# Weights' scales from column sums on TensorE, sign images for two pieces at a time

## The chip, the cores and the metric

The kernel runs on one core of a Trainium2 chip. The metric is the device time of one execution in microseconds, the median of the runs shown. The core's engines have an instruction queue each: TensorE (PE, with its weight loads shown apart as PEld), VectorE (DVE), ScalarE (ACT), GpSimd (POOL), and SyncE (SP), which issues the DMAs. TensorE writes PSUM, the others read it.

## The reference

```python
B, H, S, D, C = 4, 8, 768, 64, 16          # batch, heads, tokens, head size, clusters
# attention: a query sees only keys whose nearest centroid is its own
q_assign = argmax(einsum('bhsd,hcd->bhsc', q_n, c_n))      # the same for k
scores = where(q_assign == k_assign, (q @ k.T) / sqrt(D), -1e9)
x = softmax(scores) @ v                                    # -> (B, S, 512)
# Fourier mixing and a feed-forward layer
u = x + real(fft(fft(x, axis=1), axis=2))
un = (u - mean(u)) / sqrt(var(u) + 1e-6)
out = u + maximum(un @ w_ch1, 0) @ w_ch2                   # w_ch1 512x2048, w_ch2 2048x512
```

All inputs and the output are float32.

## The kernel before

TensorE works on 16-bit operands, so every float32 matrix is split into a high and a low half of 16 bits (`hi` and `lo`), after it was scaled by a power of two, and a product takes three matmuls.

**Attention** (class `Attention`) goes over 16 pairs of heads, four for each batch entry. A pair has six steps `st`, one for each 128 queries. `scores(pr, st)` makes two tiles `ps_big` of 128x768 in PSUM (two is all there are, so the next step has to wait until both are read): 12 matmuls (L320) and four that add the cluster mask (L325). For each of the two heads VectorE scales a tile and takes its row minimum (L339, output `ju` or, for batch 0, `X`), ScalarE takes the exponential (L345; L343 for batch 0) and its 16-bit half (L353), GpSimd the low half (L354), and SyncE transposes both by DMA into `pt` (L356). `attend` multiplies `pt` with the values into the one tile `ps_o` (L374 to L376), and every third step `finish` scales that tile into `X` on VectorE (L386, L388, L390). `prep` loads and splits q and k of a later pair in nine parts, with `along` (L48) for maxima over partitions and a one-hot code that is transposed by DMA (L303).

**Weights** (class `Weights`, the object of the change): the two matrices come in 32 pieces of 128x512, 16 each, loaded into eight buffers `RAW`, read in halves of 16 bits. Each iteration `k` of `run` does one part for several pieces:
- `load`: a DMA of 512 KB.
- `largest` (L491): VectorE takes each row's largest magnitude from the top 16 bits of the numbers; for the first matrix, four pieces' maxima are joined (L496), spread over partitions by a matmul with the identity (`along`) and reduced again (L504), so that one scale holds for four pieces; for the second each row has its own scale.
- `top_power` (L58 to L61): four small VectorE operations turn maxima into a power of two `s` and its inverse `inv`.
- `signs` (L519, L520): ScalarE makes from the top 16 bits an image of the positive numbers and one of the negative ones, in one of two buffers `PN`.
- `join` (L528, L532): two matmuls with plus and minus the identity put the images together as float32 in a tile `ps_f` (of which there are three, shared with all else but scores and `ps_o`), and VectorE adds the low bits.
- `halve`: ScalarE makes the high half (L538), and VectorE (L544) or ScalarE and GpSimd (L541, L542) the low one.

`relative` then brings the scales of both matrices together in `rel` and `dsc`.

**Fourier** and **FeedForward** follow for a finished batch entry: `fold` adds and subtracts the halves of `X` (L660) and their mirror images (L661) and splits the result; `transform` multiplies it with tables; `up` (L858) and `down` (L888) are the two products with the weights.

**Order.** `Overlap.run` writes a table of calls by step number: attention is the backbone; the 41 parts of `Weights.run` are dealt out at 0.684 steps each from step 0, the first scores come at step 5, and batch 0 ends at step 29. The Fourier and feed-forward work of entry `b` is dealt out between the steps of entry `b + 1`; that of the last entry runs by itself at the end. TensorE takes its instructions in the order of this table; on the other engines a scheduler orders them when the kernel is built.

Of the kernel before, what the change touches and what calls it, by code (L numbers as in the profile page):

```python
# [25 lines left out]
P = 128  # L26
# [28 lines left out]
def top_power(nc, tops, s, inv):  # L55

    t = tops.bitcast(I32)
    nc.vector.tensor_scalar(out=t, in0=t, scalar1=20, scalar2=None, op0=ALU.logical_shift_right)  # L58
    nc.vector.tensor_scalar(out=t, in0=t, scalar1=-910.0, scalar2=1.0, op0=ALU.add, op1=ALU.max)
    nc.vector.tensor_scalar(out=inv.bitcast(I32), in0=t, scalar1=240.0, scalar2=float(1 << 23), op0=ALU.min, op1=ALU.mult)  # L60
    nc.vector.reciprocal(out=s, in_=inv)  # L61
# [20 lines left out]
class Attention:  # L82
# [226 lines left out]
    def scores(self, pr, st):  # L309
        nc, sb = self.nc, self.sb  # L310
        assert self.ready >= pr
        (hq, hk), oh, (e, ne) = self.hl[pr], self.oht[pr], self.sc.scores(pr)
# [14 lines left out]
        for j in range(2):  # L327

            m = sb.tile([P, 1], F32, name="rmx", tag="rmx", bufs=6)
            early = pr < H // 2  # L330
            if early:

                n = (2 * st + j) % self.RING * S
                p32 = self.X[1].rearrange("p a x -> p (a x)")[:, n:n + S]
            else:
                p32 = sb.tile([P, S], F32, name="p32", tag="p32", bufs=2)
            x = p32.rearrange("p (h x) -> p h x", h=2)
            ju = x if early else sb.tile([P, 2, SH], BF16, name="ju", tag="ju")
            self.mark = nc.vector.tensor_scalar(out=ju, in0=ps[j][:, :, 0:SH], scalar1=ne, scalar2=None, op0=ALU.mult, op1=ALU.min,  # L339
                                    accum_out=m)  # L340
            self.late = m
            if early:
                nc.scalar.activation(p32, p32, AF.Exp, bias=m, scale=-1.0)  # L343
            else:
                nc.scalar.activation(x, ps[j][:, :, 0:SH], AF.Exp, bias=m, scale=e)  # L345
            if early and j:
                ph = sb.tile([P, S], F32, name="p32", tag="p32", bufs=2).bitcast(F16).rearrange("p (a x) -> p a x", a=2)
            else:
                ph = sb.tile([P, 2, S], F16, name="ph", tag="ph", bufs=2)
            if early and j and (st in self.PC):  # L350
                nc.gpsimd.tensor_copy(out=ph[:, 0], in_=p32)
            else:
                nc.scalar.copy(out=ph[:, 0], in_=p32)  # L353
            nc.gpsimd.tensor_tensor(out=ph[:, 1], in0=p32, in1=ph[:, 0], op=ALU.subtract)  # L354
# [79 lines left out]
class Weights:  # L434
# [7 lines left out]
    RAW, PN = tuple(4128 * i for i in range(6)) + (29696, 33824), (24768, 26816)  # L442
    ID, TOP, MX = 28864, 29376, 29472
# [3 lines left out]
    def __init__(self, tc, pool, arena, psf, w1, w2, ident):  # L447
# [6 lines left out]
        self.inv = [pool.tile([P, n], F32, name=f"winv{n}") for n in (4, 16)]  # L454
# [31 lines left out]
    def largest(self, k):  # L486

        nc, at = self.nc, self.arena.at
        g, i = divmod(k, 4)
        mx = at(self.MX + 32 * (g % 2), [P, 4], F32)  # L490
        nc.vector.tensor_reduce(out=mx[:, i:i + 1], in_=self.top(k).bitcast(BF16), op=ALU.max, axis=AX.X,  # L491
                                apply_absolute_value=True)
        if i == 3 and g >= 4:
            self.scales(g, mx)
        elif i == 3:
            nc.vector.tensor_reduce(out=mx[:, 0:1], in_=mx, op=ALU.max, axis=AX.X)  # L496

    def block(self, g):

        nc, at = self.nc, self.arena.at  # L500
        mx = at(self.MX + 32 * (g % 2), [P, 4], F32)
        ps = self.psf()
        along(nc, ps[:, 0:P], mx[:, 0:1], self.ident)
        nc.vector.tensor_reduce(out=mx[:, 1:2], in_=ps[:, 0:P], op=ALU.max, axis=AX.X)  # L504
        self.scales(g, mx[:, 1:2])

    def scales(self, g, mx):
        n = mx.shape[1]
        s = self.sb.tile([P, 4], F32, name="wsc", tag="wsc", bufs=2)
        top_power(self.nc, mx, s[:, 0:n], self.inv[0][:, g:g + 1] if n == 1 else self.inv[1][:, 4 * (g - 4):4 * (g - 3)])  # L510
        for i in range(4):
            self.scale[4 * g + i] = s[:, i % n:i % n + 1]

    def signs(self, k):

        nc, at = self.nc, self.arena.at
        pn = at(self.PN[k % 2], [P, 2, DM], BF16)
        top = self.top(k)
        nc.scalar.activation(pn[:, 0].bitcast(I16), top.bitcast(I16), AF.Relu, bias=self.off[:, 0:1], scale=8.0)  # L519
        nc.scalar.activation(pn[:, 1].bitcast(I16), top, AF.Relu, bias=self.off[:, 1:2], scale=8.0)  # L520
        self.bits[k] = pn
# [24 lines left out]
    def run(self):  # L546
# [5 lines left out]
        for i in range(2):  # L552
            nc.gpsimd.tensor_scalar(out=self.idb[:, i], in0=self.ident, scalar1=1.0 - 2 * i, scalar2=None, op0=ALU.mult)
        for k in range(-self.AHEAD, 33):
# [16 lines left out]
    def relative(self):  # L571

        nc, at = self.nc, self.arena.at
        top, m1, r = (at(self.TOP + 32 * j, [P, 1], F32) for j in range(3))
        rel = self.rel
        nc.vector.tensor_tensor(out=rel.rearrange("p (a c) -> p a c", c=4),
                                in0=self.inv[1].rearrange("p (a c) -> p a c", c=4),
                                in1=self.inv[0].rearrange("p (a o) -> p a o", o=1).broadcast_to([P, 4, 4]), op=ALU.mult)
        nc.vector.tensor_reduce(out=m1, in_=rel, op=ALU.max, axis=AX.X)
        ps = self.psf()  # L580
        along(nc, ps[:, 0:P], m1, self.ident)
        nc.vector.tensor_reduce(out=top, in_=ps[:, 0:P], op=ALU.max, axis=AX.X)
        nc.vector.reciprocal(out=r, in_=top)
        nc.vector.tensor_scalar(out=rel, in0=rel, scalar1=r[:, 0:1], scalar2=HSC, op0=ALU.mult, op1=ALU.mult)
# [36 lines left out]
class Fourier:  # L621
# [11 lines left out]
    FE = (0, 0, 0, 1)  # L633
# [13 lines left out]
    def fold(self, b):  # L647
# [5 lines left out]
        mid = at(self.XM, [1, M + 1], F32)  # L653
        nc.gpsimd.tensor_copy(out=mid, in_=X[0:1, 3, 0:M + 1])
        nc.gpsimd.tensor_tensor(out=mid[:, 1:M], in0=mid[:, 1:M], in1=X[0:1, 3, DM - 1:M:-1], op=ALU.add)
        last = at(self.XL, [P, 3], F32)
        xt = {}
        for i, op in self.FOLDS:
# [9 lines left out]
            xt[i] = t.rearrange("p (a t c) x -> p a t c x", a=2, t=3)  # L668
        self.parts[b] = xt, last, mid, s
# [119 lines left out]
HSC = float(2.0 ** -20)  # L789
# [111 lines left out]
class Overlap:  # L901
# [23 lines left out]
    PIN, PF, PV = (), 29, 1  # L925
    CE, WP, WQ = 0.45, 0, 0

    def layer(self, b, old):
# [13 lines left out]
        yield from old  # L942
        for blk in range(3):
            for f, cost in enumerate(ffn.up(blk)):
                if blk == 0 and f == 0:
# [116 lines left out]
def cluster_attention_fourier_ffn_kernel(ctx, tc, q, k, v, cent, w1, w2, cd, sd, cm, cs, ss, ny, out):  # L1062
# [6 lines left out]
    arena = Arena(glob, 47264)  # L1069
# [47 lines left out]
```

## Time and profile before

| | |
|---|---|
| runs | 1053.73, 1049.66, 1053.15 us; median 1053.15 |
| profiled execution | 1049.91 us, span 1048.1 us |
| busy share | TensorE 87%, VectorE 60%, ScalarE 60%, GpSimd 56% |
| mean granted TensorE clock | 0.949 |
| batch 0 beside the weights | from the first scores to the last weight piece, 31 to 192 us |
| last entry alone | from about 860 us |

Times in the profile are microseconds from the span's start. A group's row gives line, engine, operation, output and inputs with their shapes, the count, then busy time and mean ns of one, then the engine's idle time just before and what ended it. A busy engine is not always at its peak, and idle time of an engine on which nothing waits costs nothing.

### The profile page before, as it was taken

To read this page: it belongs to the slowest core of one execution; us is meant where nothing else is said; L and a number is where in the kernel's file an instruction comes from. 1 tells how busy PE (TensorE), PEld (TensorE's weight loads), DVE (VectorE), ACT (ScalarE), POOL (GpSimd) and SP (SyncE) were. 2 spreads that over 40 slices of the span, in tenths; PEclk is the share of its full clock that TensorE was granted. 3 is DMA by queue.
4 is the path that set the end of the run, shared out by engine and by line. 5 is a ranking of instruction groups with operands and counts; after the bars stand their busy time and mean duration, and the time that the engine had idled before them with its cause. 6 is when DMAs were issued, how large, how long until landed. Compare 5 with 4: busy or idle time off the path is not lost.

```text
span 1048.1 us, 23542 instructions
## 1 busy us (share of the span) xinstructions
PE 910.8 (87%) x9350; PEld 591.7 (56%) x9362; DVE 627.4 (60%) x1297; ACT 625.3 (60%) x980; POOL 586.9 (56%) x693
## 2 busy tenths in 40 slices
PE   3665565749899999998899999997999999999998
PEld 2333333425575756655666757555757667576674
DVE  8789899767757555668656555667555333631110
ACT  4798889755766665645666746556756543351230
POOL 2364565753975756655856646647847645271230
PEclk9987878769899999999899999998999999999999
DMA  7799998979887776568877767588757562321000
GB/s 272 179 225 245 196 239 166 171 156 153 177 123 153 128 154 121 121 137 161 153 137 142 140 128 132 110 141 170 124 102 133 96 110 43 81 52 31 11 11 21
DMA packets 396239, 140.01 MB, mean 134 GB/s; under 512 B 381784, under 2 KB 381792, under 8 KB 396128
## 3 DMA queue, kind: packets, MB, share of 16 engines
q1 hardware_dynamic: 396128, 138.50, 65.9%
q8 instruction: 73, 1.20, 0.5%
q14 instruction: 38, 0.31, 0.1%
HBM read 42.52 MB, written 6.29 MB: 47 GB/s over the span
## 4 chain that ended last, share of the span: by engine, by line
PE 39%; DVE 6%; DMA 3%; ACT 3%; POOL 2%; issue 2%; SPq 0%; ACTq 0%; DVEq 0%; POOLq 0%
PE ps_f L888 16%; PE ps_f L858 13%; PE ps_big L320 3%; DMA pt<-ph 3%; PE ps_f L713 2%; DVE ju L339 1%; ACT p L345 1%; PE ps_o L374 1%; POOL ph L354 1%; PE ps_o L375 1%; PE ps_o L376 1%; PE ps_big L325 1%; ACT ph L353 1%; DMA scr<-in_k_dram 0%; DVE arena L660 0%
## 5 line engine op out<-in xcount | busy, mean ns | idle before, releaser
L354 POOL TENSOR_TENSOR ph<-p,ph 128x768 f16<-128x768 f32 x144 | 242.9, 1688 | 184.6 <-ACT ph L353 150.1
L858 PE MATMUL ps_f<-arena,w1h 128*128 128x256 f16 x1536 | 271.4, 277 | 19.1 <-ACT arena L866 9.0
L888 PE MATMUL ps_f<-w2h,arena 128*128 128x512 f16 x768 | 238.9, 379 | 0.0
L345 ACT ACTIVATE p<-ps_big,rmx,sce 128x768 f32<-128x768 f32 x144 | 142.1, 988 | 132.9 <-DVE ju L339 127.5
L858 PE MATMUL ps_f<-arena,w1l 128*128 128x256 f16 x768 | 212.4, 277 | 0.0
L339 DVE TENSOR_SCALAR_CACHE_REDUCE ju<-ps_big,sce 128x768 bf16<-128x768 f32 x144 | 146.1, 1014 | 68.2 <-PE ps_big L325 58.2
L888 PEld LDWEIGHTS <-arena 128*128 128x128 f16 x1152 | 108.7, 98 | 126.6 <-issue 5.2
L858 PEld LDWEIGHTS <-w1h 128*128 128x128 f16 x1536 | 152.1, 99 | 36.0 <-issue 14.3
L867 POOL TENSOR_TENSOR arena<-arena 128x256 f16<-128x256 f32 x192 | 128.1, 677 | 77.3 <-ACT arena L866 73.6
L320 PE MATMUL ps_big<-hlk,hlq 64*128 64x384 f16 x1152 | 128.9, 348 | 39.0 <-ACT p L345 23.4
L374 PE MATMUL ps_o<-v,pt 128*128 128x66 f16 x1152 | 124.8, 198 | 43.0 <-DVE X L390 27.5
L888 PE MATMUL ps_f<-w2l,arena 128*128 128x512 f16 x384 | 145.5, 379 | 0.0
L374 PEld LDWEIGHTS <-pt 128*128 128x128 f16 x1152 | 110.2, 100 | 57.7 <-issue 37.1
L353 ACT CAST ph<-p 128x768 f16<-128x768 f32 x144 | 119.6, 832 | 15.0 <-DMA pt<-ph 12.8
L375 PE MATMUL ps_o<-v,pt 128*128 128x64 f16 x1152 | 124.8, 199 | 0.0
L376 PE MATMUL ps_o<-v,pt 128*128 128x66 f16 x1152 | 124.5, 198 | 0.0
L866 ACT ACTIVATE arena<-ps_f,wrel 128x256 f16<-128x256 f32 x192 | 90.1, 472 | 54.8 <-DVE arena L863 54.7
L863 DVE TENSOR_SCALAR arena<-ps_f,wrel 128x256 f32<-128x256 f32 x96 | 46.3, 482 | 124.9 <-PE ps_f L858 66.4
L320 PEld LDWEIGHTS <-hlq 64*128 64x128 f16 x1152 | 55.5, 99 | 101.5 <-issue 72.7
L375 PEld LDWEIGHTS <-pt 128*128 128x128 f16 x1152 | 110.7, 101 | 2.8
L376 PEld LDWEIGHTS <-pt 128*128 128x128 f16 x1152 | 111.1, 103 | 0.0
L858 PEld LDWEIGHTS <-w1l 128*128 128x128 f16 x768 | 76.1, 99 | 20.2 <-issue 10.7
(178 smaller groups left out, 1330.4 us busy)
## 6 DMA issues: line engine op xcount, KB each, us to landing
arena<-in_moe_w_ch_dram SPq DMA_DIRECT2D x32, 512.0 KB, 6.8
scr<-in_q_dram SPq DMA_DIRECT2D x16, 384.0 KB, 2.9
scr<-in_k_dram SPq DMA_DIRECT2D x16, 384.0 KB, 4.5
vst<-in_v_dram SPq DMA_DIRECT2D x16, 384.0 KB, 3.5
out_dram<-arena SPq DMA_DIRECT2D x24, 256.0 KB, 2.3
pt<-ph SPq DMA_TRANSPOSE x168, 3.9
arena<-in_cs_dram SPq DMA_DIRECT2D x12, 192.0 KB, 3.5
arena<-in_ss_dram SPq DMA_DIRECT2D x12, 192.0 KB, 3.5
```

What stands on the lines that cost most here:

```text
L320: nc.tensor.matmul(out=ps[j][:, hf, 0:SH], lhsT=hq[rows[j], a, sl], rhs=hk[rows[j], c, hs], start=(i == 0), stop=False)
L339: self.mark = nc.vector.tensor_scalar(out=ju, in0=ps[j][:, :, 0:SH], scalar1=ne, scalar2=None, op0=ALU.mult, op1=ALU.min, accum_out=m)
L345: nc.scalar.activation(x, ps[j][:, :, 0:SH], AF.Exp, bias=m, scale=e)
L353: nc.scalar.copy(out=ph[:, 0], in_=p32)
L354: nc.gpsimd.tensor_tensor(out=ph[:, 1], in0=p32, in1=ph[:, 0], op=ALU.subtract)
L374: nc.tensor.matmul(out=o[:, at:at + W], lhsT=hi, rhs=v16[:, kt, 0:W], start=(kt == 0), stop=False)
L375: nc.tensor.matmul(out=o[:, at:at + D], lhsT=hi, rhs=v16[:, kt, 66:130], start=False, stop=False)
L376: nc.tensor.matmul(out=o[:, at:at + W], lhsT=lo, rhs=v16[:, kt, 0:W], start=False, stop=(kt == ST - 1))
L858: nc.tensor.matmul(out=ps.rearrange("p (t x) -> p t x", x=P), lhsT=a[:, dc, fs], rhs=c[:, :, dc], start=(i == 0), stop=(i == 11))
L866: nc.scalar.activation(hh[:, f], ps, AF.Relu, scale=rel[:, f:f + 1])
L867: nc.gpsimd.tensor_tensor(out=hl[:, f], in0=r, in1=hh[:, f], op=ALU.subtract)
L888: nc.tensor.matmul(out=ps, lhsT=a[:, f, ts], rhs=c[:, f], start=(i == 0), stop=(i == 47))
```

## The change

**Scales.** `largest` goes. `block(g)` takes the sign images of four pieces and multiplies each (eight matmuls, two images a piece) with a matrix of ones, summing into one tile `ps_f`: each column then holds the sum of the magnitudes of that column of the four pieces, the same on all partitions. VectorE takes the largest of 512 columns, and `top_power` makes a scale from it that holds for four pieces of either matrix. Its scratch `t` now lies in PSUM, in that tile. `relative` becomes shorter, without its matmul.

**Sign images.** `signs(k)` makes the images of pieces `k` and `k + 1` in one operation each, of 1024 elements, two pieces ahead; there are three buffers of two pieces. `block` stands ahead of `join` where `k % 4 == 0`.

**Scores of batches 1 to 3.** `ju` is no tile of 16 bits in SBUF any more but the PSUM tile itself, and the exponential reads it with the constant scale -1.

**Folds.** The first of the two mirrored sums of a fold moves from GpSimd to VectorE (`FE`), and the two GpSimd operations on the middle row (`mid`) come after both folds.

`WAIT` and `N1` are new names with values that leave the order as it was; `HSC` is another constant factor.

```diff
-def top_power(nc, tops, s, inv):
-    t = tops.bitcast(I32)
-    nc.vector.tensor_scalar(out=t, in0=t, scalar1=20, scalar2=None, op0=ALU.logical_shift_right)
-    nc.vector.tensor_scalar(out=t, in0=t, scalar1=-910.0, scalar2=1.0, op0=ALU.add, op1=ALU.max)
+def top_power(nc, tops, t, s, inv):
+    t = t.bitcast(I32)
+    nc.vector.tensor_scalar(out=t, in0=tops.bitcast(I32), scalar1=23, scalar2=None, op0=ALU.logical_shift_right)
+    nc.vector.tensor_scalar(out=t, in0=t, scalar1=-13.0, scalar2=1.0, op0=ALU.add, op1=ALU.max)
     nc.vector.tensor_scalar(out=inv.bitcast(I32), in0=t, scalar1=240.0, scalar2=float(1 << 23), op0=ALU.min, op1=ALU.mult)
     nc.vector.reciprocal(out=s, in_=inv)
...
-            ju = x if early else sb.tile([P, 2, SH], BF16, name="ju", tag="ju")
+            ju = x if early else ps[j][:, :, 0:SH]
...
-            if early:
-                nc.scalar.activation(p32, p32, AF.Exp, bias=m, scale=-1.0)
-            else:
-                nc.scalar.activation(x, ps[j][:, :, 0:SH], AF.Exp, bias=m, scale=e)
+            nc.scalar.activation(x, ju, AF.Exp, bias=m, scale=-1.0)
...
     def block(self, g):
+        ps = self.psf()
+        i = 0
+        for k in range(4 * g, 4 * g + 4):
+            for j in range(2):
+                nc.tensor.matmul(out=ps, lhsT=self.ones, rhs=self.bits[k][:, j], start=(i == 0), stop=(i == 7))
+                i += 1
+        mx = at(self.MX + 32 * (g % 2), [P, 1], F32)
+        nc.vector.tensor_reduce(out=mx, in_=ps, op=ALU.max, axis=AX.X)
+        s = self.sb.tile([P, 1], F32, name="wsc", tag="wsc", bufs=2)
+        top_power(nc, mx, ps[:, 0:1], s, self.inv[g // 4][:, g % 4:g % 4 + 1])
...
     def signs(self, k):
-        pn = at(self.PN[k % 2], [P, 2, DM], BF16)
-        top = self.top(k)
+        pn = at(self.PN[k // 2 % 3], [P, 2, 2, DM], BF16)
+        raw = at(self.RAW[k % len(self.RAW)], [P, 2, 4 * DM + 16], U16)
+        top = raw[:, :, 4:4 + 4 * DM].rearrange("p a (n f) -> p a n f", f=4)[:, :, :, 0]
...
         for k in range(-self.AHEAD, 33):
-            if k >= 1 and k % 4 == 1 and k < 16:
-                self.block(k // 4)
             for p in self.loads(k):
                 self.load(p)
-            if 0 <= k + 3 < 32:
-                self.largest(k + 3)
-            if 0 <= k + 1 < 32:
-                self.signs(k + 1)
+            if k % 2 == 0 and 0 <= k + 2 < 32:
+                self.signs(k + 2)
+            if k % 4 == 0 and 0 <= k < 32:
+                self.block(k // 4)
             if 0 <= k < 32:
                 self.join(k)
...
-    FE = (0, 0, 0, 1)
+    FE = (0, 0, 0, 0)
```

TensorE before the first scores: in the kernel before, the two matmuls of the first `join` (L528) stand between the transposition of the centroid products (L271) and the maxima of pair 1 (L48 on `amx`).

```order
L271 MATMUL ps_f<-ident,ac 128x128 x3
L528 LDWEIGHTS arena
L528 MATMUL ps_f<-arena 128x512
L528 LDWEIGHTS arena
L528 MATMUL ps_f<-arena 128x512
L48 MATMUL ps_f<-ident,amx 128x128 x3
```

In the changed kernel (L491 is the matmul of `block`, L515 that of `join`) the last of eight pairs of `block` is the first below:

```order
L491 LDWEIGHTS arena
L491 MATMUL ps_f<-arena 128x512
L515 LDWEIGHTS arena
L515 MATMUL ps_f<-arena 128x512
L515 LDWEIGHTS arena
L515 MATMUL ps_f<-arena 128x512
L48 MATMUL ps_f<-ident,amx 128x128 x3
```

Eight matmuls that need the sign images of pieces 0 to 3 came ahead of the first join and of everything after it.

VectorE at the first scale, before: the last of it lies between the first reductions of scores (L339).

```order
L504 TENSOR_REDUCE arena<-ps_f 128x1
L491 TENSOR_REDUCE arena<-arena 128x1
L532 SCALAR_TENSOR_TENSOR ps_f<-arena,ps_f 128x512
L216 TENSOR_REDUCE amx<-scr 128x1
L58 TENSOR_SCALAR arena<-arena 128x1
L216 TENSOR_REDUCE amx<-scr 128x1
L59 TENSOR_SCALAR arena<-arena 128x1
L60 TENSOR_SCALAR winv_85<-arena 128x1
L61 RECIPROCAL wsc<-winv_85 128x1
L491 TENSOR_REDUCE arena<-arena 128x1
L544 SCALAR_TENSOR_TENSOR w1l<-ps_f,wsc,w1h 128x512
L339 TENSOR_SCALAR X_64,rmx<-ps_big,sce 128x768 x2
```

After (L494 is the maximum of a block's columns, L519 and L531 are L532 and L544 of before):

```order
L494 TENSOR_REDUCE arena<-ps_f 128x1
L216 TENSOR_REDUCE amx<-scr 128x1
L519 SCALAR_TENSOR_TENSOR ps_f<-arena,ps_f 128x512
L58 TENSOR_SCALAR ps_f<-arena 128x1
L59 TENSOR_SCALAR ps_f<-ps_f 128x1
L227 TENSOR_REDUCE ps_f<-ps_f 128x3
L60 TENSOR_SCALAR winv_85<-ps_f 128x1
L404 TENSOR_TENSOR ps_f<-ps_f,floor 128x3
L61 RECIPROCAL wsc<-winv_85 128x1
```

The row maxima are gone, the scale stands ahead of the first scores, and L58 to L60 work in `ps_f`.

ScalarE before the first scores, before (L235 and L199 split q, k and v; L266 is the copy that the one-hot code starts from):

```order
L519 ACTIVATE arena<-arena 128x512
L520 ACTIVATE arena<-arena 128x512
L137 ACTIVATE X_64<-X_64 128x64
L519 ACTIVATE arena<-arena 128x512
L520 ACTIVATE arena<-arena 128x512
L235 ACTIVATE hlq<-scr,scp 128x768
L235 ACTIVATE hlk<-scr,scp 128x768
L199 ACTIVATE v_230<-vst,scp 128x6x64
L199 ACTIVATE v_241<-vst,scp 128x6x64
L266 ACTIVATE ac<-ps_f,cinv 128x384
```

After (L506 and L507 are the sign operations):

```order
L137 ACTIVATE X_64<-X_64 128x64
L506 ACTIVATE arena<-arena 128x1024
L507 ACTIVATE arena<-arena 128x1024
L235 ACTIVATE hlq<-scr,scp 128x768
L235 ACTIVATE hlk<-scr,scp 128x768
L199 ACTIVATE v_230<-vst,scp 128x6x64
L199 ACTIVATE v_242<-vst,scp 128x6x64
L506 ACTIVATE arena<-arena 128x1024
L507 ACTIVATE arena<-arena 128x1024
L266 ACTIVATE ac<-ps_f,cinv 128x384
```

The signs of pieces 2 and 3 now stand ahead of L266.

More of the change, by code (lines that the diff above doesn't have):

```diff
@@ L452, in __init__ @@
         self.dsc = pool.tile([P, 1], F32, name="dsc")
-        self.inv = [pool.tile([P, n], F32, name=f"winv{n}") for n in (4, 16)]
+        self.inv = [pool.tile([P, 4], F32, name=f"winv{n}") for n in range(2)]
         self.rel = pool.tile([P, 16], F32, name="wrel")
@@ L484, in load @@
         self.nc.sync.dma_start(out=raw[:, 1:1 + 4 * DM], in_=src.bitcast(U16))
[L486 to L496, printed above, removed]
```

53 lines of the change are left out of this document (24 added, 29 removed).

## The prediction

> **What bounds the kernel now.** I read the windows of the span first (five stretches cut by what runs in them), then the list of waits in the second stretch, then single instructions there, and last the groups by line. Columns of the windows: length, then busy time and count for TensorE matmuls, TensorE weight loads, VectorE, ScalarE and GpSimd, the granted TensorE clock, the busy share of the DMA engines, GB/s.
>
> ```profile
> core 0: us, PE busy (x) PEld busy (x) DVE busy (x) ACT busy (x) POOL busy (x), PEclk, DMA share, GB/s
> 0.00:31.00 31.00, 12.95 (x52) 6.60 (x53) 25.04 (x72) 15.15 (x24) 5.54 (x38) 1.00 0.68 239
> 31.00:192.00 161.00, 98.49 (x1152) 57.32 (x1164) 138.56 (x280) 142.79 (x206) 93.38 (x79) 0.83 0.95 213
> 192.00:250.00 58.00, 39.29 (x455) 23.92 (x453) 41.97 (x80) 32.98 (x46) 32.79 (x28) 0.76 0.92 160
> 250.00:860.00 610.00, 578.69 (x6384) 382.31 (x6382) 374.97 (x772) 376.76 (x583) 389.04 (x445) 0.98 0.72 135
> 860.00:1048.00 188.00, 181.37 (x1317) 121.60 (x1313) 46.85 (x96) 57.58 (x124) 66.13 (x103) 1.00 0.16 37
> ```
>
> From 250 us to the end TensorE is busy 760.1 of 798 us, at nearly the full clock: those stretches are TensorE's. The second stretch (attention of batch 0 beside the splitting of the weights) is another kernel: TensorE is busy 98.5 of 161 us at a clock of 0.83, VectorE 138.6 (86%), ScalarE 142.8 (89%). All weight work lies in the first two stretches, and what they save comes off the end only if nothing behind them refills. The waits of the second stretch (columns: who, for whom, us in total, times, longest):
>
> ```profile
> PE ps_o L374 <- DVE X L390: 27.5, 6, 5.5
> PE ps_big L320 <- DVE X L339: 14.1, 15, 3.7
> PE ps_o L374 <- DMA pt<-p: 7.7, 6, 2.6
> ...
> ACT w2h L538 <- DVE ps_f L532: 5.8, 6, 2.7
> ACT X L343 <- DVE X L339: 4.7, 3, 2.5
> ACT w1h L538 <- DVE wsc L61: 4.6, 3, 3.0
> ```
>
> TensorE waits 41.6 of its 62.5 idle us for VectorE, and 15.1 of ScalarE's 18.2 idle us are waits for VectorE too. VectorE hands out the work here, ScalarE is the fullest. One place shows how, in order of time (start, us):
>
> ```profile
> 139.80 0.55 DVE L390 TENSOR_TENSOR X<-ps_o,rs 128x384 f32<-128x384 f32 x1
> 140.49 0.21 PE L374 MATMUL ps_o<-v,pt 128*128 128x66 f16 x1 [5.49 <-DVE X L390]
> 143.04 1.64 POOL L354 TENSOR_TENSOR ph<-X,ph 128x768 f16<-128x768 f32 x1 [1.67 <-ACT ph L353]
> 143.38 1.33 DVE L59 TENSOR_SCALAR arena<-arena 128x4 int32<-128x4 int32 x1
> 144.64 1.64 POOL L354 TENSOR_TENSOR p<-X,p 128x768 f16<-128x768 f32 x1
> 144.74 1.57 DVE L60 TENSOR_SCALAR winv<-arena 128x4 int32<-128x4 int32 x1
> ```
>
> L390, 0.55 us of work, frees the one PSUM tile of attention; it came late in VectorE's queue and TensorE stood 5.49 us. L59 and L60, on four elements, end as L354 on GpSimd ends: they stood behind it.
>
> **The change, part by part.** Groups by line (form, count | busy us, mean ns):
>
> ```profile
> L491 DVE TENSOR_REDUCE arena<-arena 128x1 f32<-128x512 bf16 x32 | 21.7, 680 | 8.0 <-DMA arena<-in_moe_w_ch_dram 7.9
> L60 DVE TENSOR_SCALAR winv<-arena 128x1 int32<-128x1 int32 (+1 forms) x8 | 6.8, 849 | 0.2
> L59 DVE TENSOR_SCALAR arena<-arena 128x1 int32<-128x1 int32 (+1 forms) x8 | 5.2, 646 | 0.1
> L227 DVE TENSOR_REDUCE ps_f<-ps_f 128x3 f32<-128x384 f32 x6 | 3.4, 561 | 2.8 <-PE ps_f L48 2.8
> L504 DVE TENSOR_REDUCE arena<-ps_f 128x1 f32<-128x128 f32 x4 | 1.1, 284 | 0.6 <-PE ps_f L48 0.6
> L408 DVE TENSOR_SCALAR ps_f<-ps_f 128x3 int32<-128x3 int32 x6 | 1.0, 168 | 0.1
> ```
>
> VectorE. Gone are 32 row maxima (21.7), four small maxima of 128x128 (1.1), and the waiting in L59 and L60: their scratch moves to PSUM, as in L408, so 12.0 becomes 16 x 0.168 = 2.7. New are eight maxima over 128x512 of PSUM; from 284 ns at 128 and 561 at 384 elements, 512 come to 0.70 us, 5.6 in all. Sum: 21.7 + 1.1 + 9.3 - 5.6 = 26.5 us less. Eight of the 32 row maxima ran before 31 us (8 x 0.68 = 5.4), so about 21 us come off in the second stretch and 5 in the first. If the PSUM form of L59 and L60 waited as before, 9.3 would be 0. The Trainium skill (SBUF — State Buffer, Who interferes with whom) says that a tensor_scalar inside SBUF can enter a mode that takes the port pair shared with GpSimd and that the later of the two then blocks for a whole instruction; the two rows at 143.38 and 144.74 agree, and by it the 9.3 us would be kept.
>
> ```profile
> L519 ACT ACTIVATE arena<-arena 128x512 int16<-128x512 int16 x32 | 24.1, 753 | 4.6 <-PE ps_f L528 1.6 <-PE ps_o L376 1.5 <-DMA scr<-in_q_dram 1.5
> L520 ACT ACTIVATE arena<-arena 128x512 int16<-128x512 uint16 x32 | 24.0, 749 | 0.0
> L343 ACT ACTIVATE X<-X,rmx 128x768 f32<-128x768 f32 x48 | 44.1, 935 | 9.3 <-DVE X L339 7.6 <-POOL ph L354 1.4 <-issue 0.3
> ...
> 125.36 0.74 ACT L519 ACTIVATE arena<-arena 128x512 int16<-128x512 int16 x1
> 126.00 0.74 ACT L520 ACTIVATE arena<-arena 128x512 int16<-128x512 uint16 x1
> ```
>
> ScalarE. 64 sign operations become 32 of 1024 elements. From 512 elements at 0.75 us to 768 at 0.935 each further 256 cost 0.185, so 1024 take 1.12 us. The next instruction starts 0.1 us before one ends (125.36 to 126.00), so the queue gains 64 x 0.65 - 32 x 1.02 = 9 us, some 8 of them in the second stretch. Bounds: 0, if the double length costs double, and 24, if length cost nothing.
>
> ```profile
> 19.19 1.06 PE L528 MATMUL ps_f<-arena 128*128 128x512 bf16 x2
> ...
> 940.18 20.72 PE ps_f L888 x96
> ```
>
> TensorE. 64 matmuls of 128x512 are new, eight for each block of four pieces. Two of them took 1.06 us at the start, so eight take about 3.6 with 0.43 for each further one; at full speed a matmul of that width takes 20.72 / 96 = 0.216, eight 1.7. That is 14 to 29 us on an engine that has 62.5 idle, so I charge nothing for the work itself; without that cover it is the whole 14 to 29. A block waits for the sign images of all its four pieces, the joins and the next step's scores stand behind it in TensorE's order, and in the order of ScalarE the last pair of signs stands ahead of the preceding step's exponentials, not right in front of the block. One PSUM tile of three stays taken until L60 has run, 4 small operations longer than before.
>
> Conversion. VectorE would be busy 138.6 - 21 = 118 us, TensorE 98.5 plus 12 to 25 (seven blocks, 111 to 124), ScalarE 142.8 - 8 = 135. ScalarE is still the fullest. At its present 89% the stretch takes 135 / 0.89 = 152 us, **9 us less**; with no waits for VectorE left it would take some 138 (135 and the 3.1 us of other waits), 23 less; if nothing follows, 0. I take 9: the nearest row is today's fill, and TensorE's own share rises from 61% to some 77% at the same time. In the first 31 us VectorE was busy 25 and loses 5, ahead of the one-hot transposition that the first scores need; TensorE's first block gives back up to 3.6. I take 1, between 0 and 3.
>
> ```profile
> L339 DVE TENSOR_SCALAR_CACHE_REDUCE ju<-ps_big,sce 128x768 bf16<-128x768 f32 x144 | 146.1, 1014 | 68.2 <-PE ps_big L325 58.2 <-ACT arena L866 2.0 <-DVE ju L339 0.9
> L345 ACT ACTIVATE p<-ps_big,rmx,sce 128x768 f32<-128x768 f32 x144 | 142.1, 988 | 132.9 <-DVE ju L339 127.5 <-POOL ph L354 5.4
> L320 PE MATMUL ps_big<-hlk,hlq 64*128 64x384 f16 x1152 | 128.9, 348 | 39.0 <-ACT p L345 23.4 <-DVE X L339 14.8 <-issue 0.7
> L532 DVE SCALAR_TENSOR_TENSOR ps_f<-arena,ps_f 128x512 uint32<-128x512 uint32 x32 | 21.5, 688 | 3.3 <-PE ps_f L528 3.2
> ```
>
> Scores of batches 1 to 3. L339 writes the scaled scores in place in PSUM, and the exponential (L345) reads them with one operand from memory less. L343, the same function with a constant scale, takes 935 against 988: 0.05 us each. It waited for L339 before as well, so no wait is added. TensorE waits 23.4 us for L345, 14 times: two exponentials shorter each time give 1.4 us; I take 1. For L339 in place, L532 writes PSUM in place at 688 ns for 512 elements, the bf16 form takes 1014 for 768; at the same ns per element L532's form would take 1032, so 0, with 0.1 us either way.
>
> ```profile
> L661 POOL TENSOR_TENSOR arena<-arena 128x765 f32<-128x765 f32 x4 | 7.2, 1808 | 5.6 <-DVE arena L660 5.6
> L661 DVE TENSOR_TENSOR arena<-arena x4: 944/1616/2277, 233.7 to 890.0; 128x765 f32<-128x765 f32 x4
> L641 ACT ACTIVATE arena<-arena,vseq 128x768 f16<-128x768 f32 x8 | 7.5, 934 | 20.9 <-DVE arena L661 8.5 <-POOL arena L661 8.0 <-DMA arena<-arena 4.5
> ```
>
> Folds. Four mirrored sums (L661) move from GpSimd (1.81 each) behind L660 on VectorE. ScalarE waited 8.0 us for the four; VectorE's form took 0.94 to 2.28, 1.61 on average (of both, ns: least, median, most), so each fold may end 0.2 us earlier, or as much as 2 where GpSimd was late, while the reductions L339 behind it on VectorE start 1.6 later. Here a rule speaks against the change: the Trainium skill (same page and section) has a VectorE instruction with two SBUF inputs contend with a GpSimd one that reads SBUF, and by it L661 stays near 2.3 wherever GpSimd has work; no row isolates it, and the sum would lose 2.8 us (4 x 0.7). I take 0. The two small GpSimd operations for the middle row come after the folds now, where only later work reads them.
>
> Sum: 9 + 1 + 1 + 0 = 11 us off the profiled execution's 1049.9 (span 1048.1 and 1.8 around it), **1039 us**. The three runs are 1049.7, 1053.2 and 1053.7; the profile is like the fastest. For the median I put 1040.
>
> **Rivals.**
> - *ScalarE fills up, and TensorE stays warm.* TensorE's clock in the second stretch was 0.83 on average, 1.00 from 860 us on; denser work there may raise it, which shortens scores and attention as well. With ScalarE's queue free of waits for VectorE the stretch loses 23, in all 25: 1025. The Trainium skill (TensorE: Matmul & The Clock Gate, Part 1) gives two clocks, half and full, and the full one after some 3.4 us of sustained work; a clock of 0.83 over 161 us is a mixture that fits.
> - *The gain is eaten by DMA and the loop of a step.* The DMA share is 0.95, and transpositions alone keep the engines full:
>
> ```profile
> 813.00:815.00 2.00, 2.00 (x24) 1.00 (x22) 0.04 (x1) 1.93 (x4) 1.12 (x2) 1.00 1.04 195
> ```
>
>   One transposition of `pt` fills 2 us at 195 GB/s. The stretch runs about 42 of them (two for each of 21 steps, 84 us) and 24 weight pieces of 512 KB, which at the 239 GB/s of the first window take 2.2 us each (53 us): 137 of 161 us. Against it, TensorE's waits for `pt` are 7.7 us, those for VectorE 41.6. If it holds, the gain is 0 to 5: 1048.
> - *The block stalls TensorE: slower.* If the last signs are late, joins and scores stand still for them, ScalarE then gets no scores, and everything waits in a ring. Idle TensorE time is 62.5 / 8 = 7.8 us for each block; a block that costs 3.6 and waits over 5.6 us more (7.8 + 11 / 8 - 3.6) turns the gain into a loss; at 8 us of wait the time is about 1050 + 8 x 2.4 = 1069. Against it: the order on ScalarE has the signs ahead.
> - *The in-place reduction is dearer.* At +0.5 us on each of 2 L339 in the 14 steps where TensorE waits, 14 us: 1053.
> - *The change does not do what it says* would be row maxima or L59's waits still there: the order excludes the first.
>
> **How the numbers follow.** Forecast 0.53 (1033 to 1044), warm and full 0.14 (1023 to 1033), DMA 0.20 (1045 to 1053), stall 0.08, in-place 0.05. The likeliest gives 1040. From 1024 to 1054 all but the stall, half of the in-place case and the lowest tail are in, 0.87; nearer ends would cut into the DMA case. About 0.5% of 1053 (5.3 us) is what runs here can tell from no change: faster means below 1047.9. Forecast, the warm case and two fifths of the DMA case: 0.75; the rest of that and some of the in-place case 0.14; slower than 1058.4: 0.11.
>
> **What would show it.** Right: the second stretch shrinks by about 9 us, TensorE's waits for L390 and L339 there fall from 41.6 to under 25, L59 and L60 take under 0.25 us each, signs take 1.1 us, VectorE is busy some 26 us less in the first 192 us, the stretch from 250 us on keeps its length. Wrong: TensorE waits for sign images at the block's matmuls for more than 10 us in all; waits for `pt` grow by what those for VectorE lose; L339 in place takes over 1.1 us; or the second stretch shrinks and the third grows by the same.

## The result and the profile after

The kernel after takes **1061.5 us** (median of 7 runs, 1058.2 to 1062.3) against 1052.8 for the kernel before (7 runs, 1049.7 to 1055.5): ratio **1.0077, 95% interval 1.0057 to 1.0097**. It is slower by some 8 us; I had forecast 13 us faster, with 1054 as the upper end. The profiled execution has a span of 1060.3 us at a mean clock of 0.937, against 1048.1 at 0.949.

The same five windows in the kernel after (columns as in the prediction):

```profile
0.00:31.00 31.00, 13.80 (x59) 7.16 (x61) 21.90 (x68) 18.44 (x25) 5.69 (x39) 0.94 0.69 239
31.00:192.00 161.00, 104.64 (x1137) 56.38 (x1154) 117.08 (x249) 130.48 (x168) 89.76 (x77) 0.78 0.96 212
192.00:250.00 58.00, 35.40 (x426) 23.05 (x428) 43.25 (x69) 31.82 (x43) 31.62 (x25) 0.74 0.76 141
250.00:860.00 610.00, 575.53 (x6309) 378.48 (x6307) 377.81 (x775) 363.40 (x584) 387.13 (x444) 0.98 0.70 134
860.00:1048.00 188.00, 186.22 (x1437) 126.73 (x1436) 52.98 (x109) 62.49 (x131) 69.03 (x107) 1.00 0.20 43
```

In the second stretch VectorE, ScalarE and GpSimd are all less busy than before, and TensorE is busier by 6 us (the window has a fixed length, and since the attention steps came later it also holds a little less of their work). What TensorE waits for there has changed hands:

```profile
PE ps_o L371 <- DMA pt<-p: 25.0, 12, 6.8
PE ps_big L320 <- DVE X L339: 10.4, 10, 3.1
PE ps_o L371 <- DMA pt<-ph: 6.1, 6, 3.3
PE ps_f L263 <- ACT arena L528: 3.2, 1, 3.2
```

Waits for VectorE (L390 and L339) fell from 41.6 to 10.4 us; one of 5.8 us for L387, the L390 of before, ends at 192.9 us, just behind the window. Waits for `pt` rose from 11.8 to 31.1. The groups that the change touches:

```profile
L494 DVE TENSOR_REDUCE arena<-ps_f 128x1 f32<-128x512 f32 x8 | 5.4, 680 | 10.2 <-PE ps_f L491 10.2
L59 DVE TENSOR_SCALAR ps_f<-ps_f 128x1 int32<-128x1 int32 x8 | 1.3, 163 | 0.1
L60 DVE TENSOR_SCALAR winv<-ps_f 128x1 int32<-128x1 int32 x8 | 1.2, 155 | 0.2
L506 ACT ACTIVATE arena<-arena 128x1024 int16<-128x1024 int16 x16 | 19.5, 1217 | 10.8 <-PE ps_f L515 9.2 <-DMA arena<-in_moe_w_ch_dram 1.1 <-PE ps_big L325 0.4
L507 ACT ACTIVATE arena<-arena 128x1024 int16<-128x1024 uint16 x16 | 19.2, 1203 | 0.0
L491 PE MATMUL ps_f<-arena 128*128 128x512 bf16 x60 | 22.0, 516 | 1.2 <-issue 0.7 <-DVE oh L289 0.2 <-DVE hlq L236 0.2
L342 ACT ACTIVATE p<-ps_big,rmx 128x768 f32<-128x768 f32 x144 | 128.9, 900 | 131.5 <-DVE ps_big L339 117.4 <-POOL ph L351 5.8 <-POOL rpow L825 3.3
L339 DVE TENSOR_SCALAR_CACHE_REDUCE ps_big<-ps_big,sce 128x768 f32<-128x768 f32 x144 | 141.5, 1020 | 44.5 <-PE ps_big L325 44.4
```

Nearly every single price came out near its estimate. To see where the time went I took the start of each attention step (its first L339; steps are counted from 0, batch 0 has 24) and cut the windows there. From the span's start to the start of step 22, of before and then of after:

```profile
0.00:196.67 196.67, 115.25 (x1275) 66.55 (x1287) 167.06 (x358) 161.36 (x233) 101.97 (x121) 0.86 0.91 215
```

```profile
0.00:205.79 205.79, 127.35 (x1341) 69.96 (x1362) 148.28 (x332) 155.81 (x201) 104.87 (x124) 0.81 0.88 207
```

TensorE was busy 12.1 us longer and idle 3.0 us less: 9.1 us late at step 22, 9.6 at step 28 and 14.3 at step 48; the profiled spans differ by 12.2 us in the end, the medians of the runs by 8.7. The kernel after was ahead by 10.9 us at step 12 (114.7 against 125.6). Steps 12 and 13 then took 27.6 us instead of 11.6, and steps 14 to 21 another 4.0 us more than before. The first long waits stand at 120 and 132 us (start, us, engine, line; in order of time):

```profile
114.10 0.92 ACT L342 ACTIVATE X<-X,rmx 128x768 f32<-128x768 f32 x1
114.93 0.82 ACT L350 CAST ph<-X 128x768 f16<-128x768 f32 x1
115.65 1.26 ACT L525 ACTIVATE w2h<-ps_f,wsc 128x512 f16<-128x512 f32 x2
116.80 0.69 ACT L528 ACTIVATE arena<-ps_f,wsc 128x512 f32<-128x512 f32 x1
117.37 0.94 ACT L235 ACTIVATE hlq<-scr,scp 128x768 f16<-128x768 f32 x1
118.20 0.94 ACT L235 ACTIVATE hlk<-scr,scp 128x768 f16<-128x768 f32 x1
119.02 0.83 ACT L350 CAST p<-X 128x768 f16<-128x768 f32 x1
...
123.24 1.86 SPq L481 DMA_DIRECT2D arena<-in_moe_w_ch_dram  x2
125.69 0.33 SPq L210 DMA_DIRECT2D scr<-in_q_dram  x1
126.12 2.03 SPq L353 DMA_TRANSPOSE pt<-p  x1
...
132.42 0.24 PE L371 MATMUL ps_o<-v,pt 128*128 128x66 f16 x1 [6.78 <-DMA pt<-p]
```

The second exponential ended at 115.0. Its cast came at 119.0, behind halves of weights and the splits of q and k for a later pair; then the transposition stood in SP's queue behind two weight loads that waited for a join, and that join stood behind the waiting attention on TensorE. The first theories were made from these rows.

### The profile page after: what moved, and what is told of

Same layout as the page of the kernel before. It is cut to its first block, busy times and chain, and to the rows that moved or that the text cites. A ratio compares the mean times of both kernels' runs of the same rounds, so it can differ in the third digit from the quotient of the medians.

```text
span 1060.3 us, 23581 instructions
## 1 busy us (share of the span) xinstructions
PE 923.7 (87%) x9396; PEld 595.3 (56%) x9416; DVE 613.8 (58%) x1268; ACT 606.6 (57%) x948; POOL 583.2 (55%) x690
## 4 chain that ended last, share of the span: by engine, by line
PE 42%; DVE 18%; DMA 13%; POOL 9%; ACT 9%; issue 7%; SPq 1%; ACTq 0%; POOLq 0%; DVEq 0%
PE ps_f L872 16%; PE ps_f L842 13%; DVE ps_big L339 4%; POOL ph L351 4%; DMA pt<-ph 4%; PE ps_big L320 3%; DMA pt<-p 3%; ACT ph L350 3%; DMA vst<-in_v_dram 2%; PE ps_o L371 1%; POOL arena L851 1%; PE ps_o L373 1%; PE ps_o L372 1%; ACT p L342 1%; PE ps_f L697 1%
## 5 line engine op out<-in xcount | busy, mean ns | idle before, releaser
L351 POOL TENSOR_TENSOR ph<-p,ph 128x768 f16<-128x768 f32 x144 | 243.2, 1697 | 183.9 <-ACT ph L350 146.5
L342 ACT ACTIVATE p<-ps_big,rmx 128x768 f32<-128x768 f32 x144 | 128.9, 900 | 131.5 <-DVE ps_big L339 117.4
L339 DVE TENSOR_SCALAR_CACHE_REDUCE ps_big<-ps_big,sce 128x768 f32<-128x768 f32 x144 | 141.5, 1020 | 44.5 <-PE ps_big L325 44.4
L320 PE MATMUL ps_big<-hlk,hlq 64*128 64x384 f16 x1152 | 126.0, 346 | 38.8 <-ACT p L342 22.3
L373 PE MATMUL ps_o<-v,pt 128*128 128x66 f16 x1152 | 124.7, 198 | 0.0
L842 PEld LDWEIGHTS <-w1l 128*128 128x128 f16 x768 | 75.9, 99 | 22.5 <-issue 13.3
```

The costliest lines, as they stand in the source:

```text
L320: nc.tensor.matmul(out=ps[j][:, hf, 0:SH], lhsT=hq[rows[j], a, sl], rhs=hk[rows[j], c, hs], start=(i == 0), stop=False)
L342: nc.scalar.activation(x, ju, AF.Exp, bias=m, scale=-1.0)
L373: nc.tensor.matmul(out=o[:, at:at + W], lhsT=lo, rhs=v16[:, kt, 0:W], start=False, stop=(kt == ST - 1))
L842: nc.tensor.matmul(out=ps.rearrange("p (t x) -> p t x", x=P), lhsT=a[:, dc, fs], rhs=c[:, :, dc], start=(i == 0), stop=(i == 11))
```

## Experiments

Theories: **A**, `pt` is late in SP's queue, behind loads that wait; **B**, TensorE pays for the block matmuls; **C**, scores or folds cost what was lost; **D**, the DMA engines are full; **E**, weights' work on ScalarE, in bursts or ahead of the casts, makes the steps late. Behind each time stands its ratio to the kernel before, run in the same session, with the 95% interval.

**e1, the weights' part alone.** In after: `ju` a 16-bit tile (in a free part of the weights' memory) and `scale=e` again, `FE = (0, 0, 0, 1)` again, with `mid` ahead of the folds.

> The kernel after with the scores and the folds put back as before (the junk tile of L339 lies in a part of the arena that is free from batch 1 on, for room); only the weights' part of the change is left. Three theories are open. A, order: the new order lets a transposition of pt stand in SP's queue behind a weight load that waits for a join, and the join stands behind the waiting attention on TensorE; the loss is in the weights' part: about 1061 us (1057 to 1065). B, TensorE pays: the 64 block matmuls are not covered by idle time; also in the weights' part: about 1061. C, scores or folds: in-place scores or folds on VectorE cost what was lost after 192 us: about 1043 (1036 to 1048).

1060.5 us, 1.0079 (1.0049 to 1.0109). The loss is in the weights' part; C is out as its main cause.

**e2, the scores' part alone; e3, the folds' part alone**, each put into before.

> The kernel before with the scores' part alone: L339 writes in place in PSUM, the exponential reads that with a constant scale. A and B expect 1052 us (a gain of 1, within 3 us of before's 1053). C expects 1058 or more if the scores are its cause.

> The kernel before with the folds' part alone: the four mirrored sums on VectorE, the two small GpSimd operations behind the folds. A and B expect 1053 us (within 3 us of before). C expects 1058 or more if the folds are its cause.

e2: 1055.7 us, 1.0034 (1.0015 to 1.0054), a small loss. e3: 1052.7, 1.0004 (0.9985 to 1.0022), nothing.

**e4, two block matmuls instead of eight.**

```diff
-        for k in range(4 * g, 4 * g + 4):
-            for j in range(2):
-                nc.tensor.matmul(out=ps, lhsT=self.ones, rhs=self.bits[k][:, j], ...)
+        for j in range(2):
+            nc.tensor.matmul(out=ps, lhsT=self.ones, rhs=self.bits[4 * g + 3][:, j], ...)
```

> The kernel after with two matmuls for each block instead of eight: only the sign images of the block's last piece are summed, so the scale is that of one piece in four. The waits for signs stay, 48 matmuls of 128x512 go (at the 0.35 to 0.52 us measured, 17 to 25 us of TensorE time). A: the work was in idle time, so 1061 us, at most 4 less. B: what was added comes off again: 1045 to 1050. C: 1061.

1062.1 us, 1.0098 (1.0062 to 1.0133): no gain. Up to step 22 TensorE was busy 112.5 us, 15 less than in after, and idle 85.3, 7 more; the rest was lost again by step 28 (254.1 us, 3.5 ahead of after, from 8.0 at step 22) and later. Taking the work away does not give its time back, as B would have it (1045 to 1050).

**e5, weight loads one piece later**: `k == p - (len(self.RAW) - 2)` in `loads`. **e10**, the same in before.

> The kernel after with each weight piece's load issued one piece later (six pieces ahead instead of seven), so that the buffer it fills was freed by a join a whole piece ago and the load should no longer hold SP's queue. Bytes are the same. A (a transposition of pt stands in SP's queue behind a load that waits for a join): TensorE's waits for pt in 31 to 205 us fall from 31 to under 15, time 1045 to 1053 us. D (the DMA engines are full, share 0.95, and pt is late by bandwidth): no change, 1058 to 1064. E (the weights' work now comes to ScalarE in bursts of two or four pieces, and the casts and exponentials of the steps wait behind it): no change, 1058 to 1064.

> Control: the kernel before with the loads one piece later. In it VectorE, not pt, held TensorE, so A expects no change: 1050 to 1055 us. If later loads are worth 7 us in any order of the work: 1043 to 1048.

e5: 1054.2 us, 1.0013 (0.9994 to 1.0033): some 7 us come back. e10: 1053.5, 1.0012 (0.9996 to 1.0028), no gain in before. That looked like A, but waits for `pt` only fell from 31.1 to 24.5 us (31 to 205 us), not under 15.

**e6 and e7, half loads** for 24 of 32 pieces, in after and in before; both kernels leave out the other half of these pieces' numbers.

```diff
-        self.nc.sync.dma_start(out=raw[:, 1:1 + 4 * DM], in_=src.bitcast(U16))
+        c = 4 * DM if k < len(self.RAW) else 2 * DM
+        self.nc.sync.dma_start(out=raw[:, 1:1 + c], in_=src.bitcast(U16)[:, 0:c])
```

> The kernel after with 24 of the 32 weight pieces loaded by half (256 KB instead of 512, the other half of the buffer stays as it was): 6.3 MB less, at the 210 GB/s of the stage some 29 us of DMA time. All instructions, waits and places in the queues stay, but for the scheduler's answer to shorter loads. D: the stage shortens by 15 to 29 us, 1032 to 1046 us. A: the waits in SP's queue are for a join, not for bytes: 1055 to 1062. E: 1058 to 1064.

> The same edit in the kernel before, as a control: if its stage is handed out by VectorE and not by DMA (my reading in the prediction), 1048 to 1053 us; if DMA limits that stage too (D for both kernels), 1030 to 1043.

e6: 1051.2 us, 0.9982 (0.9961 to 1.0003). e7: 1055.6, 1.0031 (1.0012 to 1.0051): the kernel before got a little slower with 6.3 MB less, against 1048 to 1053 expected. e6 lies outside the ranges of all three theories: it gave back what after had lost and no more. e5 and, below, e14 and e18 come within 3 us of it with all bytes moved, and in e14 the DMA engines are fuller up to step 22 (0.94) than in after (0.88). So D, which would have had e6 at 1032 to 1046, does not explain the lost 9 us.

**e8, sign images piece by piece**: `signs(k + 3)` in each turn, 64 operations of 512 elements.

> The kernel after with the sign images made piece by piece again (64 operations of 512 elements, one piece in each turn of the weights' loop, three pieces ahead), block sums and scales as in after. ScalarE gets back 9 us of work but in even portions. E: 1045 to 1054 us. A and D: 1058 to 1065.

1057.8 us, 1.0045 (1.0026 to 1.0063): somewhat less than half of the loss back with 9 us more work on ScalarE, just outside the ranges of E and of A and D.

**e9, e1 with the loads of e5; e12, e5 with the blocks of e4.**

> Experiment e1 (only the weights' part of the change) with the loads of experiment e5 (one piece later). If the parts add up (scores alone cost 3.6 us, loads issued later give back 7): 1048 to 1052 us, the best version so far and not above the kernel before. If the gain of later loads was only another throw of the scheduler's order: 1053 to 1060.

> Experiment e5 (after, loads later) with two matmuls a block instead of eight (the scale is that of one piece in four): 48 matmuls less, about 12 us of TensorE time by what e4 showed. If TensorE's added work is paid once pt is no longer late (B, which e4 did not show): 1043 to 1049 us. If it lies in idle time: 1052 to 1056.

e9: 1051.5 us, 1.0016 (0.999 to 1.0041). e12: 1059.9, 1.0088 (1.0065 to 1.0112): 48 matmuls less, 5.6 us slower than e5, and above both ranges. Neither A nor B explains that. An edit changes the durations that the scheduler counts with when the kernel is built, and so the order on every engine but TensorE; e12 has other orders than e5 on all of them.

**e11, scores into SBUF**: `ju = x` for all batches, on e2.

> Experiment e2 (scores alone) with L339's output in SBUF, in the tile that the exponential writes anyway (as batch 0 has it), instead of in place in PSUM: PSUM is free when L339 ends, not when the exponential ends. If what the scores' part costs is the write and the read of the same PSUM tile: 1048 to 1053 us, TensorE's 22 us of waits for the exponential (L320) under 8. If VectorE is then held by GpSimd, which reads the two buffers of that tile: 1058 or more.

1060.2 us, 1.0081 (1.0061 to 1.0101). TensorE's wait stayed as long, now for VectorE, which itself waits for GpSimd (6.8 us) to free the tile:

```profile
PE ps_big L320 <- DVE p L339: 23.4, 12, 4.5
```

**e13, casts first.** Here only the order changes. In batch 0, what `weights` and `prep` issue on ScalarE stands behind the last cast of the step before (a slot is a step's place in the table of calls):

```diff
+                self.cast = nc.scalar.copy(out=ph[:, 0], in_=p32)
...
+            with self.tc.issue_after(c.ins):     # c: the last cast when this slot began
                 next(wgen, None)                 # the same around the parts of prep
```

**e14**, the same for the slots of steps 11 to 13 alone; **e15**, e13's rule in before.

> The kernel after with one rule more for ScalarE's queue in batch 0: what the weights and the preparation of the next pair issue in a slot stands behind the last cast (L350) of the slot before. No work changes. Order theory (signs, halves and splits ahead of the casts make pt late): TensorE's waits for pt in 31 to 205 us fall from 31 to under 18, time 1047 to 1054 us. If the lateness only moves to the joins and halves: 1057 to 1064.

> The same rule for three slots alone (steps 11 to 13), the place of the two longest waits of after (5.4 and 6.8 us for pt at 120 and 132 us). If these two waits are what the change lost: 1050 to 1056 us, and step 14 starts at 137 us or earlier, not 142. If the time is lost again in the next steps: 1058 to 1063.

> Control: the rule of e13 in the kernel before, where VectorE and not pt held TensorE. Order theory: 1049 to 1057 us, no gain. If the rule is good in any order: 1042 to 1047.

e13: 1053.6 us, 1.001 (0.9988 to 1.0032). e14: 1053.3, 1.0016 (0.9998 to 1.0034). e15: 1055.3, 1.0019 (1.0000 to 1.0038). The order alone gives back 8 us in after by the medians, 6 to 7 by the ratios, and nothing in before. Waits for `pt` fell only to 22.5 us in e13 and 26.8 in e14 (31 to 205 us), less than I expected. In e14 (one line more in the code, so line numbers are one higher), ScalarE at the same place, and the window to step 22:

```profile
112.67 0.82 ACT L351 CAST ph<-X 128x768 f16<-128x768 f32 x1
113.39 0.68 ACT L526 ACTIVATE w2h<-ps_f,wsc 128x512 f16<-128x512 f32 x1
113.97 0.82 ACT L351 CAST p<-X 128x768 f16<-128x768 f32 x1
114.69 1.23 ACT L507 ACTIVATE arena<-arena 128x1024 int16<-128x1024 int16 x1
```

```profile
0.00:191.08 191.08, 125.98 (x1361) 67.19 (x1362) 144.77 (x329) 155.30 (x201) 102.35 (x122) 0.86 0.94 222
```

The cast stands 1.3 us behind its sister, not 4.1, and step 22 starts at 191.1, with TensorE as busy as in after and idle 13 us less.

**e16, e13's rule on e9; e17, e14's rule on e1; e18, e14's rule on after, but for steps 16 to 18**, as a placebo: a rule at a place that, by the theory, should not matter.

> The rule of e13 on experiment e9 (weights' part alone, loads later), the best version so far (1051.5). If casts first and loads later act on different waits: 1043 to 1049 us, faster than before. If both mend the same waits: 1050 to 1054.

> The rule of e14 (three slots, steps 11 to 13) on experiment e1 (the weights' part alone, 1060.5 us). If e14 mends what the weights' part costs and the scores' part costs 3.6 us beside it: 1047 to 1051 us. If the scores' part is free once the order is mended: 1052 to 1055. If e14 was one lucky order: 1056 to 1062.

> Placebo for e14: the same rule on after for three later slots (steps 16 to 18), so that ScalarE's order up to step 15 stays as in after. If the order at steps 11 to 13 is the cause, the waits of 5.4 and 6.8 us at 120 and 132 us stay, step 14 starts at 142 us, time 1056 to 1062 us. If any new order of the queue gives the 8 us back: 1050 to 1055.

e16: 1051.8 us, 1.0000 (0.9979 to 1.0021). e17: 1050.4, 0.998 (0.9957 to 1.0003), the best, and not distinguishable from before. e18: **1051.6, 0.9987 (0.9968 to 1.0006)**: the placebo worked as well as the cure. Its waits at 122 and 134 us stayed (2.9 and 6.6 us) and its step 14 started at 142.1, as in after; the time came back later. TensorE even waited for `pt` as long as in after, 31.2 us in the second stretch (31 to 192 us) against 31.1:

```profile
PE ps_o L372 <- DMA pt<-p: 24.6, 12, 6.6
PE ps_big L321 <- DVE X L340: 10.2, 11, 2.7
PE ps_o L372 <- DMA pt<-ph: 6.6, 5, 2.6
```

So a kernel with after's waits for `pt` can be level with before, and these waits, on which A and E rest, do not explain the loss. Steps 14 to 21, up to the start of step 22, in after and in e18:

```profile
142.35:205.79 63.44, 40.25 (x470) 22.86 (x476) 48.22 (x97) 46.10 (x60) 37.05 (x31) 0.78 0.73 157
```

```profile
142.13:193.82 51.69, 37.72 (x464) 20.34 (x461) 41.24 (x93) 45.40 (x60) 32.84 (x29) 0.87 0.93 190
```

The same steps take 63.4 us or 51.7. TensorE's idle time is 23.2 us or 14.0; its busy time is 2.5 us longer in after, at a granted clock of 0.78 instead of 0.87. VectorE is busy 7.0 us longer in after; part of that is work that e18 does behind the cut, 2.4 us are two instructions (L201) that met GpSimd:

```profile
185.25 1.64 POOL L351 TENSOR_TENSOR ph<-X,ph 128x768 f16<-128x768 f32 x1 [1.57 <-ACT ph L350]
185.66 3.55 DVE L201 SCALAR_TENSOR_TENSOR v<-vst,scp,v 128x384 f16<-128x384 f32 x2
186.86 1.95 POOL L351 TENSOR_TENSOR p<-X,p 128x768 f16<-128x768 f32 x1
192.21 0.55 DVE L387 TENSOR_TENSOR X<-ps_o,rs 128x384 f32<-128x384 f32 x1
192.90 0.21 PE L371 MATMUL ps_o<-v,pt 128*128 128x66 f16 x1 [5.82 <-DVE X L387]
```

The same two instructions in e18:

```profile
179.81 0.61 DVE L202 SCALAR_TENSOR_TENSOR v<-vst,scp,v 128x384 f16<-128x384 f32 x1
...
180.93 0.61 DVE L202 SCALAR_TENSOR_TENSOR v<-vst,scp,v 128x384 f16<-128x384 f32 x1
```

L201 took 1.8 us on average instead of 0.61 while L351 ran on GpSimd; L387, 0.55 us of work, came behind it and 3 us of other work in VectorE's queue, and TensorE stood 5.8 us. By the Trainium skill (SBUF — State Buffer, Who interferes with whom) a VectorE instruction with two SBUF inputs contends with a GpSimd one that reads SBUF; these rows agree. But TensorE stood 6.1 us for the same instruction in e5 (at 181 us) and 6.3 in e13 (at 186), and both are level with before: this wait alone is not the loss either.

## Why the prediction was wrong

| us | step 14 starts | step 22 | step 28 | step 48 | TensorE busy / idle to step 22 |
|---|---|---|---|---|---|
| before | 137.2 | 196.7 | 247.9 | 419.0 | 115.3 / 81.4 |
| after | 142.4 | 205.8 | 257.5 | 433.3 | 127.4 / 78.4 |
| e1 | 144.3 | 207.3 | 260.9 | 434.0 | 126.4 / 80.9 |
| e5 | 137.7 | 191.9 | 244.8 | 421.3 | 124.7 / 67.2 |
| e9 | 143.4 | 196.6 | 249.4 | 422.2 | 126.3 / 70.3 |
| e13 | 140.5 | 196.3 | 249.0 | 427.3 | 129.7 / 66.5 |
| e14 | 135.5 | 191.1 | 245.5 | 421.1 | 126.0 / 65.1 |
| e16 | 139.6 | 195.0 | 244.9 | 417.6 | 126.7 / 68.3 |
| e17 | 137.6 | 192.6 | 245.5 | 417.7 | 127.1 / 65.5 |
| e18 | 142.1 | 193.8 | 247.4 | 423.7 | 126.8 / 67.0 |

The starts are microseconds from the span's start. Each row is one profiled execution, and the runs of one kernel lie several us apart (e14: 1048.9, the profiled one, to 1057.0), so a difference of 2 or 3 us between two rows proves nothing by itself.

**Right: the prices.** The weights' groups on VectorE took 26.9 us less (26.5 forecast), and it was busy 24.6 less in the first 192 us. L59 and L60 went from 12.0 us to 2.5 (2.7). That agrees with the rule of the Trainium skill named there (SBUF — State Buffer, Who interferes with whom). The eight maxima took 0.68 us each (0.70), a sign operation 1.21 (1.12), L339 in place 1.02 (1.03); the first scores came 1.3 us earlier (1); the folds were worth nothing (e3).

**Wrong: the step "Conversion".** It took the fill of the fullest engine as fixed: ScalarE would keep its 89%, and 135 us of its work would therefore take 152. In after the fill did not stay. ScalarE fell to 130.5 of 161 us, 81%; over the same steps, up to step 22, it fell from 161.4 of 196.7 us (82%) to 155.8 of 205.8 (76%). Those steps became 9.1 us longer, where the stretch was to lose 9. In e14 and e18 the same work in another order had a fill of 81% and 80%, and step 22 came 5.6 and 2.9 us earlier than in before. A busy share does not say which of these orders a build will get. A step of batch 0 goes from TensorE through VectorE, ScalarE, GpSimd and SP back to TensorE, and TensorE attends in a fixed order; the time hangs on when each link is served. What was won at step 22 did not last, either: at step 28 the faster orders lie between 3.1 us ahead of before (e5) and 1.5 behind (e9). The prediction had named this condition ("only if nothing behind them refills") and put no price on it.

**Not borne out: "I charge nothing for the work itself"**, the term of TensorE, put beside 62.5 idle us. To step 22 TensorE was busier than in before by 9 to 15 us in all kernels of the table with the block sums. Its idle time fell by 0.5 to 3 us in after and e1, and by 11 to 16 in the others. So in the better orders what was added and what idle time gave up nearly cancel: they win 0 to 6 us up to step 22, not 9, and after's order loses 9. Whether the added matmuls cost their time, or other waits took the place of those for VectorE, these sums do not tell. That the work can be sold back is not so: e4 and e12 took three quarters of it away and gained nothing. What the runs do show is that idle time made of waits in a chain cannot be entered as free room without a trial.

**Wrong: the scores' term, "I take 1".** e2 lost 3.6 us (1.6 to 5.7). e14 against e17 and e5 against e9, the same weights' part with and without it (and the folds), give 2.9 and 2.8 by the medians; by the ratios the second pair shows nothing (1.0013 and 1.0016), nor does after against e1. The traces are clearer. The place is steps 28 to 48: 171.1 us in before, 172.2 in e17 and 173.1 in e1, but 175.3 to 176.5 in e2, after, e5, e14 and e18. Over all traces it is 174.4 to 178.3 us with the scores' part and 170.4 to 173.1 without. TensorE's idle time ahead of `up` there is 2.5 us in before, 3.1 in e17, 5.0 in e2 and 5.4 in e14, the largest part of it for ScalarE's output of `up`. One unlisted instruction got dearer: the read of the row minimum behind each L339, in before and then in e2:

```profile
L339 DVE DVE_READ_ACCUMULATOR ju<-ps_big,sce 128x1 f32 x144 | 11.9, 83 | 0.0
```

```profile
L339 DVE DVE_READ_ACCUMULATOR ps_big<-ps_big,sce 128x1 f32 x144 | 20.3, 141 | 0.0
```

That is 8.4 us more of VectorE over three batches. That it is the cause of those waits was not tried, and e11, where this read is as cheap as in before, needed 177.4 us for the same steps, with other waits.

**The rivals.** I wrote that it would be a wrong sign if "waits for `pt` grow by what those for VectorE lose"; they grew by 19.3 of 31.2. I had tied that to full DMA engines and a gain of 0 to 5, and e6, e7 and e14 do not bear that out. TensorE did not get warmer, my case for a larger gain: its clock in the second stretch fell from 0.83 to 0.78, and up to step 22 it was 0.86 in e14, as in before. The stall of TensorE at the blocks, my only slower case, did not come: L491 waited 1.2 us in all. Missing was the rival that decided: a change of the work gives every engine but TensorE a new order, and the order by itself was worth 10 us here (after against e18). Kernels with the weights' part took 1050.4 to 1062.1 us; those without it, e11 apart, 1051.7 to 1055.7. The kernel after lies at the bad end of its band, and the good end is level with before: even there the forecast gain of 13 us is missing.

**What stays open.** e13, e14 and e18 changed nothing but the order, so that after's order costs 6 to 10 us against theirs is shown. Which feature of it does is not: e14 mended the place of the longest waits, e18 left it and mended a later one, and both came out level, since a new order at one place also shifts what meets later (ScalarE's order in e14 differs from after's in the steps behind 14 as well). The late cast, the loads in SP's queue and the meeting of L201 with L351 are links that the rows show, not a sum that adds up to the loss. Open, too, is why the better orders win nothing in the end: up to step 22 the added TensorE work nearly cancels what the waits gave up, and the scores' part costs some 3 us more, but no run separates the two.

## What to carry to other kernels

Where a stretch is a ring of engines in which each waits for the next, do not count the idle time of one engine as free room for more work, and doubt any gain that comes from a busy share. Where a scheduler sets the order at build time, treat each edit as a new draw: before believing a gain or a loss of a per cent, build the same work in two or three other orders (a constraint on one queue, a load issued a piece later) and compare the bands. A placebo costs one more kernel, and here it kept a wrong story from being told.

## What was unexpected

- Two VectorE instructions of 0.61 us took 1.65 and 1.99 us beside GpSimd's subtraction, and a wait of 5.8 us on TensorE followed.
- The read of an accumulated minimum took 141 ns behind a reduction that writes float32 into PSUM, 83 behind one that writes 16 bits into SBUF and 82 behind one that writes float32 into SBUF.
- The exponential over 768 elements of PSUM took 988 ns with a scale from memory, 900 with a constant one, and 931 with a constant one from SBUF: the term I had put at 0.05 us was 0.09, and no gain from it shows in the time.
